# Turning slot rows in place, and the upper heads from 128 B runs, on VectorE instead of TensorE, in a windowed-attention and mixture-of-experts kernel

## The chip, the cores and the metric

The kernel runs on one core of a Trainium2 chip. The metric is device time in microseconds (us). Before the change three runs gave a median of 631.35 us (630.63 to 631.54). The engines are named as the profile names them: PE (TensorE; PEld is its weight load), DVE (VectorE), ACT (ScalarE), POOL (GpSimd) and SP (SyncE, which here only starts transfers). Each has a queue of its own that it works through in order.

## The reference, cut to what matters

```python
# attention: q, k, v are [8 batches, 8 heads, 576 positions, 64]
scores = np.matmul(q, k.transpose(0, 1, 3, 2)) / 8
mask = (rel >= 0) & (rel < 64)               # rel = query position - key position
attn = softmax(np.where(mask, scores, -1e9))
x = np.matmul(attn, v)                       # heads put side by side: [4608, 512]
# mixture of experts: w1 is [8, 512, 1024], w2 is [8, 1024, 512]
logits = x @ w_gate + modality_bias[modality_id]
e_idx = np.argmax(logits, axis=1)
gate_w = softmax(logits)[arange, e_idx]
for e in range(8):
    rows = e_idx == e
    out[rows] = gate_w[rows, None] * (np.maximum(x[rows] @ w1[e], 0) @ w2[e])
```

## The kernel before, in words

**Attention.** The 4608 positions are 72 blocks of 64; two blocks are a *pair* (36 pairs, 128 query rows each), two pairs a *group* (18 groups of four blocks). The main loop `for s in range(NPR + 4)` (L1023) takes one pair a step and holds, written out by hand, the stages of several pairs: scores, minima (L637), exponentials (L649), the turns of the probabilities (`probs_t`, L481), the values (L675), `values_out` (L681 and L683, rows `xa`), the turn of those rows, the logits (L700, and L705, which adds the bias: `lg`) and the route, which scatters each row by its expert into the DRAM tensor `xs_scratch`.

Scores need Q and K with the head dimension on the partitions. They arrive with positions on the partitions, and *heads are turned*: step s turns those of group s//2 + 1, K at even s and Q at odd s, in two parts, `heads[0]` (heads 0 to 3, L1076 to L1079) and `heads[1]` (heads 4 to 7, L1098 to L1101). A part is four PE turns of 128x128 (`heads_t`, through `turn`, L481) into a bank named `tp`, then one copy into `kT` or `qT` (`heads_out`, L588): by ACT for the second part of K, by DVE otherwise. `load_qk` (L563) brings a group's q or k in two transfers of 256 B runs (L574), or in four where the group straddles two batches (groups 11, 13 and 15 among those that matter here). Groups 1 to 7 are loaded ahead into a stock; from 8 on, the loads are issued on SP three steps (k) or two steps (q) ahead of the turns, into two rotating buffers.

**Experts.** Routed rows are processed in *slots* of 256 rows, 18 of them and a half one at the end. A slot needs its rows turned too: x with its 512 columns on the partitions, split into a rounded high part `xh` (ACT, L195) and the rest `xl` (DVE, L196), since each product is made of three matmuls (high by high, low by high, high by low; the weights are split alike into `Whi`, L114 on ACT, and `Wlo`, L119 on DVE, from pieces that SP loads into `y`, L103). `first` (L318) makes the hidden layer, of which ACT takes `hh` (L326) and DVE `hl` (L327); `second` (L340) makes the output `y`, which DVE scales (L348) and POOL scatters (L351).

A generator, `slot_pieces`, cuts a slot into 16 pieces of matmuls. From step FIRST = 12 on, each attention step has four gaps, and `gap` puts one piece into each, so that a slot takes four steps, and PE's order alternates between attention and experts. What ACT and DVE do behind a piece is put into the list `later`, and `run_later` writes it out at fixed places of the step. Behind attention the remaining pieces follow each other (`last` is set).

The next slot's rows are fetched by `fetch` (L250) into `xt`, one buffer, ahead of the piece `first(2, 1)`. Eight slots, the first, six more beside attention and the one just behind it, come by one transfer with rows on the partitions, and PE turns them: `x_turn` (L266, L281), eight turns of 128x128, four into bank `em` ahead of one piece and four into bank `tp` behind another; `x_split` (L285) then makes `xh` and `xl` from PSUM. The seven after the first start their turns at 114.5, 158.1, 201.8, 245.9, 289.4, 331.5 and 361.8 us of the span. The other ten and the half slot, fetched when attention is over, come in *quarters*: four transfers, each 32 partitions wide, and a fifth for the tail (gate weight and row number), so that 32x32 blocks need only be turned in themselves, which is what DVE's transpose does (L276, 128x256 at a time, into PSUM).

PSUM banks are in pools: `tp` is a pool of two (`ps_t`), taken in turn by the head turns, the probability turns, the logits and the slots' second half; `em`, `y0`, `y1`, `sp0` have one bank each.

Of the kernel before, what the change touches and what calls it, by code (L numbers as in the profile page):

```python
# [19 lines left out]
P = 128  # L20
W64 = 64
# [5 lines left out]
def tile_window_attn_moe(  # L27
# [28 lines left out]
    TP = 2 * P  # L56
# [18 lines left out]
    NC1 = DM // P  # L75
# [118 lines left out]
    def split(ps, hi, lo):  # L194
        nc.scalar.copy(out=hi, in_=ps)  # L195
        nc.vector.tensor_tensor(out=lo, in0=ps, in1=hi.bitcast(F32), op=ALU.subtract)  # L196
# [32 lines left out]
    last = []  # L229
    position = [-4]  # L230
# [19 lines left out]
    def fetch():  # L250
        if fetched:
            return fetched.pop(0)
        row, late, buf, whichever, need = todo.pop(0)
        assert late is not None or not pads
        assert late is None or late in scattered
        tick(need - issued[0], table=True)
        nb = 1 if whichever == NANY else 2
        quarters = bool(last)
        xt = load_slot(row, late, nb, quarters)
        return dict(xt=xt, buf=buf, any=whichever, nb=nb, quarters=quarters,  # L260
                    tail=tail_of(xt) if quarters else xt[:, :, DM:])

    def slot_pieces():


        def x_turn(sl, i, tp=None):  # L266

            xt, nb = sl["xt"], sl["nb"]
            if ("tp", i) in sl or nb == 1 and i == 0:
                return  # L270
            tp = sl["tp", i] = tp or bank(2 if i and (last or not sl["quarters"]) else 0)
            cs_ = range(2 * i, 2 * i + 2) if nb == 2 else range(NC1)
            for n, c in enumerate(cs_):
                cols = slice(n * nb * P, (n + 1) * nb * P)
                if sl["quarters"]:
                    nc.vector.transpose(  # L276
                        out=tp[:, cols].rearrange("p (w t) -> p w t", t=R32),
                        in_=x_of(xt)[:, 0:nb, :, :, c].rearrange("p b w d -> p (b w) d"))
                    continue
                for t in range(nb):  # L280
                    nc.tensor.transpose(  # L281
                        out=tp[:, cols][:, t * P:(t + 1) * P].bitcast(F32R),
                        in_=xt[:, t, c:DM:NC1].bitcast(F32R), identity=ident_r)

        def x_split(sl, i):  # L285

            nb = sl["nb"]
            x_turn(sl, i)
# [4 lines left out]
            hi, lo = (x[:, (2 * i * TP if nb == 2 else 0):][:, 0:512] for x in sl["x"])
            split(sl.pop(("tp", i)), hi, lo)
            if i == 1:
                sl["gate"] = epool.tile([P, 2], F32, name="gate", bufs=2)
                nc.gpsimd.tensor_copy(out=sl["gate"][:, 0:nb], in_=sl["tail"][:, 0:nb, 0])
                sl["id"] = epool.tile([P, 2], I32, name="id", bufs=2)
                nc.gpsimd.tensor_copy(out=sl["id"][:, 0:nb], in_=sl["tail"][:, 0:nb, 1])

        def x_part(sl, i, tp=None):
            if not sl["quarters"]:
                x_turn(sl, i, tp)
            later.append(lambda: x_split(sl, i))
# [107 lines left out]
        NK = NC2 // 2  # L412
# [10 lines left out]
        while True:  # L423
            nxt = None
            for k in range(1, NK):
                for i in range(2):
                    if (k, i) == ((1, 0) if last else (2, 1)) or k == 2 and i == 1 and nxt is None:
                        assert todo
                        nxt = fetch()
                    first(sl, k, i)  # L430
                    if k == NK - 1 and i == 0 and last and nxt["quarters"]:
                        later.append(lambda: (x_turn(nxt, 0), x_turn(nxt, 1)))
                    yield
                for t in range(2):
# [69 lines left out]
    def by_group(x):  # L504
        return x.rearrange("p (a h j) i -> p a h j i", a=2, h=HP)
# [49 lines left out]
    def new_qk(G, nm):  # L555
# [4 lines left out]
        else:  # L560
            qk[G, nm] = work.tile([P, 2, H, D], F32, name="qk", bufs=2)

    def load_qk(G, nm, blocks=range(GBLK), dma=nc.sync):  # L563

        t = qk[G, nm]
        x = q if nm == "q" else k
        i = blocks[0]
        while i <= blocks[-1]:
            b, g = divmod(GBLK * G + i, BPB)
            n = min(BPB - g, blocks[-1] + 1 - i)  # L570
            src = x[b, :, g * W64:(g + n) * W64].rearrange("h (p t) d -> p t h d", t=2)
            p0 = i * W64 // 2
            for par in range(2):
                dma.dma_start(out=t[p0:p0 + n * W64 // 2, par], in_=src[:, par])  # L574
            i += n

    def heads_t(G, nm, i, tp):


        src = qk[G, nm].rearrange("p t (h a) d -> p t h (a d)", a=2)  # L580
        for h in range(2):
            for t in range(2):
                n = 2 * h + t
                turn(tp[:, n * P:(n + 1) * P], src[:, t, 2 * i + h])
# [438 lines left out]
    for s in range(NPR + 4):  # L1023
# [70 lines left out]
        if n_gap > 2:  # L1094
            if FIRST <= s < FIRST + 4:
                weights(s)
            gap(it, True)
        if heads:  # L1098
            tp = turn_bank(s)
            heads_t(G, *heads[1], tp)  # L1100
            heads_out(tp, G, *heads[1], nc.scalar.copy if heads[1] == K1 else nc.vector.tensor_copy)  # L1101
# [283 lines left out]
```

## Time and profile before

| | before |
|---|---|
| median of three runs | 631.35 us |
| the profiled execution, of which the profile is | 630.53 us |
| its span, first to last instruction | 628.8 us |
| mean granted TensorE clock | 0.999 |
| PE busy | 611.0 us (97%) |
| DVE busy | 383.9 us (61%) |
| ACT busy | 296.8 us (47%) |
| POOL busy | 136.1 us (22%) |
| DMA | 150230 packets, 88.07 MB |

A row of a group reads: line, engine, operation, output tile <- input tiles, partitions x elements and type, number; then busy time and the mean of one in ns; then the engine's idle time just ahead of these, and what ended most of it. A row of a timeline has the start in us and the duration in us of what stands behind it (xN: N instructions in a row, first start to last end), and in brackets the wait ahead of it and its releaser. Matmuls overlap in the records, so PE is read from start to start. SPq rows are transfers being issued; the time is that of the issuing, not of the data. The chain of waits gives: waiter <- releaser: us, times, longest.

### The profile page before, as it was taken

How to read it: one execution, taken by the hardware profiler on the slowest of the kernel's cores; microseconds unless marked ns; L12 is line 12 of the kernel's file. 1: busy time of each engine (PE TensorE's matmuls, PEld its weight loads, DVE VectorE, ACT ScalarE, POOL GpSimd, SP SyncE). 2: the span in 40 equal slices, each digit the busy share in tenths (PEclk: the TensorE clock that was granted, in tenths of full speed). 3: DMA queues.
4: the chain of work that ended last, by engine and by line, in shares of the span. 5: the costliest groups of instructions: out<-in, count | busy, mean ns of one | idle time of the engine just before them, and what ended most of it. 6: DMA issues, size and time to landing. Idle time of an engine off the chain costs nothing. (4 is left out here: it accounts for less than half of the span.)

```text
span 628.8 us, 17271 instructions
## 1 busy us (share of the span) xinstructions
PE 611.0 (97%) x6429; PEld 549.2 (87%) x6429; DVE 383.9 (61%) x1493; ACT 296.8 (47%) x933; POOL 136.1 (22%) x315
## 2 busy tenths in 40 slices
PE   8899799999999999999999999999999999999996
PEld 5788688989898899989898899999899999989986
DVE  4899878766676765656655266324434743876721
ACT  4899785656556554645553111111113522564411
POOL 5423412222222320320323130011011011101102
PEclk9999999999999999999999999999999999999999
DMA  9999846675467544452412132732332653578300
GB/s 177 220 240 242 236 123 181 173 200 171 111 163 194 143 120 103 136 152 60 127 53 85 51 102 71 217 118 67 85 118 76 191 165 96 190 244 252 112 11 27
DMA packets 150230, 88.07 MB, mean 140 GB/s; under 512 B 120010, under 2 KB 130816, under 8 KB 150016
## 3 DMA queue, kind: packets, MB, share of 16 engines
q1 hardware_dynamic: 141568, 67.45, 41.6%
q0 software_dynamic: 5888, 18.93, 8.0%
q8 instruction: 51, 0.84, 0.5%
q10 hardware_dynamic: 2688, 0.58, 0.5%
q14 instruction: 35, 0.29, 0.2%
HBM read 67.49 MB, written 23.91 MB: 145 GB/s over the span
## 5 line engine op out<-in xcount | busy, mean ns | idle before, releaser
L340 PE MATMUL y<-Whi,hh 128*128 128x512 f32 x288 | 117.0, 406 | 0.0
L649 ACT ACTIVATE ss<-ss,mn 128x128 f32<-128x128 f32 x288 | 112.6, 398 | 2.0 <-DVE mn L637 2.0
L340 PE MATMUL y<-Wlo,hh 128*128 128x512 f32 x288 | 112.7, 391 | 0.0
L340 PE MATMUL y<-Whi,hl 128*128 128x512 f32 x288 | 112.6, 391 | 0.0
L351 POOL DMA_INDIRECT out_dram<-y,id x36 | 37.4, 1040 | 248.3 <-DVE y L348 165.4
L327 DVE SCALAR_TENSOR_TENSOR hl<-em,hh 128x512 fp32r<-128x512 f32 x50 | 34.5, 690 | 92.3 <-ACT hh L326 89.6
L318 PE MATMUL em<-xh,Whi 128*128 128x256 f32 x400 | 83.7, 291 | 0.0
L326 ACT ACTIVATE hh<-em 128x512 fp32r<-128x512 f32 x50 | 29.6, 593 | 106.1 <-PE em L318 102.1
L318 PE MATMUL em<-xl,Whi 128*128 128x256 f32 x400 | 79.3, 279 | 0.0
L318 PE MATMUL em<-xh,Wlo 128*128 128x256 f32 x400 | 79.2, 279 | 0.0
L637 DVE CUSTOM_DVE_ANT_0 ss<-sp,masks 128x128 f32<-128x128 f32 x288 | 63.6, 286 | 11.9 <-PE sp L623 10.5
L658 ACT COPY pT<-tp 128x512 f32<-128x512 f32 x57 | 31.4, 590 | 74.7 <-PE tp L481 74.0
L340 PEld LDWEIGHTS y<-Whi,hl 128*128 128x128 f32 x288 | 54.1, 188 | 12.2
L318 PEld LDWEIGHTS em<-xh,Whi 128*128 128x128 f32 x400 | 62.3, 189 | 2.0 <-DVE xl L196 0.2
L340 PEld LDWEIGHTS y<-Whi,hh 128*128 128x128 f32 x288 | 54.2, 188 | 8.2
L340 PEld LDWEIGHTS y<-Wlo,hh 128*128 128x128 f32 x288 | 54.2, 188 | 7.8
L318 PEld LDWEIGHTS em<-xl,Whi 128*128 128x128 f32 x400 | 60.9, 188 | 0.0
L318 PEld LDWEIGHTS em<-xh,Wlo 128*128 128x128 f32 x400 | 60.9, 188 | 0.0
L649 ACT ACTIVATION_READ_ACCUMULATOR ss<-ss,mn 128x1 f32 x288 | 56.1, 195 | 0.0
L776 POOL DMA_INDIRECT xs_scratch<-xa,idx x36 | 36.4, 1012 | 82.5 <-DVE lm L719 27.2
L326 ACT ACTIVATE hh<-sp 128x512 fp32r<-128x512 f32 x22 | 13.2, 598 | 76.0 <-PE sp L318 74.0
L675 PEld LDWEIGHTS av<-ve,pT 128*64 128x64 f32 x576 | 36.3, 138 | 12.1 <-issue 5.7
(251 smaller groups left out, 1231.0 us busy)
## 6 DMA issues: line engine op xcount, KB each, us to landing
vo<-in_v_dram SPq DMA_DIRECT2D x32, 256.0 KB
y<-in_moe_w_dram SPq DMA_DIRECT2D x32, 256.0 KB
vo<-in_moe_w_dram SPq DMA_DIRECT2D x24, 256.0 KB
ss<-in_moe_w_dram SPq DMA_DIRECT2D x24, 256.0 KB
xt<-xs_scratch SPq DMA_DIRECT2D x40, 128.0 KB
xt<-xs_scratch SPq DMA_DIRECT2D x8, 514.0 KB
xs_scratch<-xs_scratch SPq DMA_DIRECT2D x8, 514.0 KB
pT<-in_moe_w_dram SPq DMA_DIRECT2D x16, 256.0 KB
```

Of the source, the lines that this page charges most:

```text
L318: nc.tensor.matmul(out=hb[:, i * TP:(i + 1) * TP], lhsT=w[buf][:, c0:c0 + P], rhs=x[:, c * TP:(c + 1) * TP], start=(n == 0), stop=(n == le ...
L326: nc.scalar.activation(out=hh, in_=hb, func=AF.Relu),
L327: nc.vector.scalar_tensor_tensor(out=hl, in0=hb, scalar=0.0, in1=hh.bitcast(F32), op0=ALU.max, op1=ALU.subtract)))
L340: nc.tensor.matmul(out=sl["y", t], lhsT=h[:, i * TP + t * P:i * TP + (t + 1) * P], rhs=w[buf][:, c0:c0 + DM], start=(k == 0 and n == 0), s ...
L351: ins = nc.gpsimd.indirect_dma_start(out=out, out_offset=bass.IndirectOffsetOnAxis(ap=sl["id"][:, t:t + 1], axis=0), in_=y, in_offset=None ...
L637: nc.vector.tensor_tensor_reduce(out=ss[a][:, hp, :], in0=sp[a][:, hp * P:(hp + 1) * P], in1=mask, scale=-1.0 / 8.0, scalar=3.0e38, op0=AL ...
L649: nc.scalar.activation(out=ss[a][:, hp, :], in_=ss[a][:, hp, :], func=AF.Exp, bias=mn[:, h:h + 1], scale=-1.0, accum_out=sm[:, h:h + 1])
L658: nc.scalar.copy(out=pT, in_=pp)
L675: nc.tensor.matmul(out=av[c * W64:(c + 1) * W64, 2 * hp + a], lhsT=pT[:, i:i + W64], rhs=(vo if c else ve)[p][:, 2 * hp + a, :], start=Tru ...
L776: ins = nc.gpsimd.indirect_dma_start(out=xs, out_offset=bass.IndirectOffsetOnAxis(ap=idx[:, j:j + 1], axis=0), in_=xg[j], in_offset=None)
```

## The change

**Slot rows.** `quarters` is now true for every slot but the first, so the seven slots named above also load by five transfers instead of one. PE no longer turns their rows. `x_turn` turns a whole slot in place in `xt`, SBUF to SBUF, by two DVE transposes of 128x512; it is queued in `later` behind `first(3, 1)` (in the tail, where DVE turned already, behind `first(3, 0)`). `xh` and `xl` are made from `xt` and no longer from PSUM.

**Heads.** For groups 8 to 17 (QUARTERS = 8; turned at steps 14 to 33) heads 0 to 3 are loaded and turned as before, from one half of the tile. Heads 4 to 7 are loaded into its other half by eight transfers, one for each head and 32-column half, each 32 partitions wide in runs of 128 B. `turn_heads` then makes `kT` or `qT` by a single DVE transpose of 128x512, in the place where four PE turns and a copy stood. A q or k load is ten transfers instead of two, twenty instead of four where the group straddles two batches.

```diff
-        quarters = bool(last)
+        quarters = bool(position[0] > 0)
...
-        def x_turn(sl, i, tp=None):
+        def x_turn(sl):
+            blocks = x_of(sl["xt"])[:, 0:sl["nb"]].rearrange("p b w d c -> p (b w) c d")
+            for c in range(0, NC1, 2):
+                nc.vector.transpose(out=blocks[:, :, c:c + 2], in_=blocks[:, :, c:c + 2])
...
+            if sl["quarters"]:
+                tp = x_of(xt)[:, 0:nb].rearrange("p b w t c -> p c (b w) t")[:, cs_]
+                hi, lo = (x.rearrange("p (c w t) -> p c w t", w=nb * NR, t=R32) for x in (hi, lo))
+            else:
+                tp = tp or bank(2 if i else 0)
...
-                    if k == NK - 1 and i == 0 and last and nxt["quarters"]:
-                        later.append(lambda: (x_turn(nxt, 0), x_turn(nxt, 1)))
+                    if k == NK - 1 and i == (0 if last else 1) and nxt["quarters"]:
+                        later.append(lambda: x_turn(nxt))
...
+    QUARTERS = 8
...
+    def turn_heads(G, nm, i):
+        dst = by_group(qT if nm == "q" else kT)[:, G % 2, 2 * i:2 * i + 2]
+        nc.vector.transpose(
+            out=dst.rearrange("p h j i -> p (h j i)"),
+            in_=by_heads(qk[G, nm]).rearrange("p h u d -> p (h u d)"))
...
+            nh = H if G < QUARTERS else HP
...
+            for h in range(nh, H):
+                for c in range(2):
+                    rows = slice((h % 2 * 2 + c) * R32, (h % 2 * 2 + c + 1) * R32)
+                    src = x[b, h, g * W64:(g + n) * W64, c * R32:(c + 1) * R32]
+                    dma.dma_start(out=by_heads(t)[rows, (h - nh) // 2, u, :],
+                                  in_=src.rearrange("(u p) d -> p u d", p=R32))
...
-        if heads:
+        if heads and G >= QUARTERS:
+            turn_heads(G, *heads[1])
+        elif heads:
             tp = turn_bank(s)
             heads_t(G, *heads[1], tp)
```

How this moves instructions is shown at the fifth of the seven slots that change (its turns start at 289.4 us before). Lines behind the change are numbered anew: L340 is L334 after, L327 is L321, L705 is L723, L574 is L585 and L591. DVE before; `cnt`, `tgt`, `se`, `dst` and the two reciprocals are the route's, `xl` the slot's low part:

```order
L327 SCALAR_TENSOR_TENSOR hl<-em,hh 128x512
L801 COPY cnt<-tp 1x8
L757 TENSOR_TENSOR tgt<-tp,ebase 128x16
L588 COPY qT<-tp 128x2x2x128
L762 TENSOR_REDUCE se<-ex 128x2
L763 TENSOR_TENSOR tgt<-tgt,oh 128x16
L764 TENSOR_SCALAR se<-se 128x2
L766 TENSOR_REDUCE dst<-tgt 128x2
L770 RECIPROCAL xa_102<-se 128x1
L770 RECIPROCAL xa_103<-se 128x1
L196 TENSOR_TENSOR xl<-em,xh 128x512
L196 TENSOR_TENSOR xl<-tp,xh 128x512
```

DVE in the same place after:

```order
L321 SCALAR_TENSOR_TENSOR hl<-em,hh 128x512
L270 STREAM_TRANSPOSE xt<-xt 128x8x2x32 x2
L819 COPY cnt<-tp 1x8
L775 TENSOR_TENSOR tgt<-tp,ebase 128x16
L569 STREAM_TRANSPOSE qT<-qk 128x512
L780 TENSOR_REDUCE se<-ex 128x2
L781 TENSOR_TENSOR tgt<-tgt,oh 128x16
L782 TENSOR_SCALAR se<-se 128x2
L784 TENSOR_REDUCE dst<-tgt 128x2
L788 RECIPROCAL xa_102<-se 128x1
L788 RECIPROCAL xa_103<-se 128x1
L196 TENSOR_TENSOR xl<-xt,xh 128x512 x2
```

Two slot turns stand ahead of the route's small operations, the copy of Q has become a turn, and both `xl` read `xt`. Behind both come `rs`, `xa` and `lg` (L681, L683 and L705 before). On PE, at the same slot, before (`y_5162` and `y_5181` are two output banks of the experts; the numbers only tell tiles apart):

```order
L340 MATMUL y_5162<-Whi_2480,hh 128x512
L340 MATMUL y_5162<-Wlo_67,hh 128x512
L340 MATMUL y_5162<-Whi_2480,hl 128x512
L481 MATMUL tp<-ident_r,qk 128x128 x4
L281 MATMUL em<-ident_r,xt 128x128 x4
L340 MATMUL y_5181<-Whi_2480,hh 128x512
L340 MATMUL y_5181<-Wlo_67,hh 128x512
L340 MATMUL y_5181<-Whi_2480,hl 128x512
```

PE there after:

```order
L334 MATMUL y_5255<-Whi_2505,hh 128x512
L334 MATMUL y_5255<-Wlo_67,hh 128x512
L334 MATMUL y_5255<-Whi_2505,hl 128x512
L334 MATMUL y_5269<-Whi_2505,hh 128x512
L334 MATMUL y_5269<-Wlo_67,hh 128x512
L334 MATMUL y_5269<-Whi_2505,hl 128x512
```

The turns of the second pair of heads and the first four of the slot are gone, and one piece follows the other. On SP, group 11's k load (it straddles two batches), between a load of v and the expert weights, before:

```order
L103 DMA y<-in_moe_w_dram 128x512
L539 DMA vo<-in_v_dram 128x8x64
L574 DMA qk<-in_k_dram 32x8x64 x2
L574 DMA qk<-in_k_dram 96x8x64 x2
L103 ISA
L103 DMA y<-in_moe_w_dram 128x512
```

The same place on SP after:

```order
L103 DMA y<-in_moe_w_dram 128x512
L534 DMA vo<-in_v_dram 128x8x64
L585 DMA qk<-in_k_dram 32x4x64 x2
L591 DMA qk<-in_k_dram 32x2x32 x8
L585 DMA qk<-in_k_dram 96x4x64 x2
L591 DMA qk<-in_k_dram 32x6x32 x8
L103 ISA
L103 DMA y<-in_moe_w_dram 128x512
```

Four issues became twenty, and the next piece of weights stands behind all of them.

More of the change, by code (lines that the diff above doesn't have):

```diff
@@ L263, in slot_pieces, with x_part @@
     def slot_pieces():
-        def x_turn(sl, i, tp=None):
-            xt, nb = sl["xt"], sl["nb"]
[L269 to L288, printed above, removed]
+        def x_turn(sl):
+            blocks = x_of(sl["xt"])[:, 0:sl["nb"]].rearrange("p b w d c -> p (b w) c d")
+            for c in range(0, NC1, 2):
+                nc.vector.transpose(out=blocks[:, :, c:c + 2], in_=blocks[:, :, c:c + 2])
+        def x_part(sl, i, tp=None):
+            xt, nb = sl["xt"], sl["nb"]
             if i == 0:
@@ L292, in x_split, with out_ @@
                     return
[L293 to L304, printed above, removed]
+            cs_ = slice(2 * i, 2 * i + 2) if nb == 2 else slice(0, NC1)
+            hi, lo = (x[:, cs_.start * nb * P:][:, 0:512] for x in sl["x"])
+            if sl["quarters"]:
[3 more added lines that the diff above has]
+                tp = tp or bank(2 if i else 0)
+                for n, (c, t) in enumerate((c, t) for c in range(cs_.start, cs_.stop) for t in range(nb)):
+                    nc.tensor.transpose(
+                        out=tp[:, n * P:(n + 1) * P].bitcast(F32R), in_=xt[:, t, c:DM:NC1].bitcast(F32R),
+                        identity=ident_r)
+            def out_():
+                split(tp, hi, lo)
+                if i == 1:
+                    sl["gate"] = epool.tile([P, 2], F32, name="gate", bufs=2)
+                    nc.gpsimd.tensor_copy(out=sl["gate"][:, 0:nb], in_=sl["tail"][:, 0:nb, 0])
+                    sl["id"] = epool.tile([P, 2], I32, name="id", bufs=2)
+                    nc.gpsimd.tensor_copy(out=sl["id"][:, 0:nb], in_=sl["tail"][:, 0:nb, 1])
+            later.append(out_)
         def first(sl, k, i):
@@ L561, in new_qk, with plain, by_heads @@
             qk[G, nm] = work.tile([P, 2, H, D], F32, name="qk", bufs=2)
+    def plain(t, nh):
+        return t.rearrange("p t h d -> p (t h d)")[:, 0:2 * nh * D].rearrange("p (t h d) -> p t h d", t=2, d=D)
+    def by_heads(t):
+        return t.rearrange("p t h d -> p (t h d)")[:, H * D:].rearrange("p (h u d) -> p h u d", h=HP // 2, d=R32)
+    def turn_heads(G, nm, i):
[3 more added lines that the diff above has]
+            in_=by_heads(qk[G, nm]).rearrange("p h u d -> p (h u d)"))
     def load_qk(G, nm, blocks=range(GBLK), dma=nc.sync):
@@ L570, in load_qk @@
             n = min(BPB - g, blocks[-1] + 1 - i)
-            src = x[b, :, g * W64:(g + n) * W64].rearrange("h (p t) d -> p t h d", t=2)
+            nh = H if G < QUARTERS else HP
+            src = x[b, 0:nh, g * W64:(g + n) * W64].rearrange("h (p t) d -> p t h d", t=2)
             p0 = i * W64 // 2
             for par in range(2):
-                dma.dma_start(out=t[p0:p0 + n * W64 // 2, par], in_=src[:, par])
+                dma.dma_start(out=plain(t, nh)[p0:p0 + n * W64 // 2, par], in_=src[:, par])
+            u = slice(i * W64 // R32, (i + n) * W64 // R32)
+            for h in range(nh, H):
[4 more added lines that the diff above has]
+                                  in_=src.rearrange("(u p) d -> p u d", p=R32))
             i += n
     def heads_t(G, nm, i, tp):
-        src = qk[G, nm].rearrange("p t (h a) d -> p t h (a d)", a=2)
+        src = plain(qk[G, nm], H if G < QUARTERS else HP).rearrange("p t (h a) d -> p t h (a d)", a=2)
         for h in range(2):
```

## The prediction

> **What bounds the kernel now.** I read the page first, then the busy time by stretches, then the timelines of TensorE (PE), VectorE (DVE), ScalarE (ACT) and the SP queue around the instructions that change. The page's sums:
>
> ```profile
> PE 611.0 (97%) x6429; PEld 549.2 (87%) x6429; DVE 383.9 (61%) x1493; ACT 296.8 (47%) x933; POOL 136.1 (22%) x315
> ```
>
> Busy time by stretches, one with attention and one behind it (columns: span, then PE, PEld, DVE, ACT, POOL, granted clock, DMA share, GB/s):
>
> ```profile
> 230.00:275.00 45.00, 44.98 (x575) 40.82 (x575) 28.36 (x151) 24.95 (x92) 10.76 (x22) 1.00 0.45 120
> 400.00:480.00 80.00, 80.00 (x519) 72.80 (x519) 29.52 (x45) 12.46 (x23) 8.71 (x23) 1.00 0.37 107
> ```
>
> PE has no idle time worth the name in either, and the clock is full. So work taken off PE shortens the run, unless another queue then makes PE wait. DVE is busy 63% of the attention stretch (28.36 of 45), in order, and receives nearly all the new work; that is where I look for the wait.
>
> **What a turn costs PE.** Four turns of a Q or K tile (L481), then the y matmuls; a step without slot turns:
>
> ```profile
> 278.41 0.60 PE L481 MATMUL tp<-ident_r,qk 128*128 128x128 f32 x4
> 278.76 0.48 PE L340 MATMUL y<-Whi,hh 128*128 128x512 f32 x1
> 279.08 0.40 PE L340 MATMUL y<-Wlo,hh 128*128 128x512 f32 x1
> 279.31 0.40 PE L340 MATMUL y<-Whi,hl 128*128 128x512 f32 x1
> ```
>
> PE is read by start times, because busy times overlap. The four turns hold it 0.35 us (278.41 to 278.76), and the matmul behind them takes 0.32 instead of 0.23 to its successor, so four turns cost 0.44. The second pair of heads is taken off PE for k and q of ten groups: 20 x 0.44 = 8.8 us. Now a step in which a slot's rows are turned too (I call it an x-step; this is the fifth of the seven that change):
>
> ```profile
> 288.84 0.39 PE L340 MATMUL y<-Whi,hl 128*128 128x512 f32 x1
> 289.07 0.60 PE L481 MATMUL tp<-ident_r,qk 128*128 128x128 f32 x4
> 289.42 0.74 PE L281 MATMUL em<-ident_r,xt 128*128 128x128 f32 x4
> 290.00 0.46 PE L340 MATMUL y<-Whi,hh 128*128 128x512 f32 x1
> ...
> 291.46 0.63 PE L281 MATMUL tp<-ident_r,xt 128*128 128x128 f32 x4
> 292.02 0.27 PE L675 MATMUL av<-ve,pT 128*64 128x64 f32 x1
> ...
> 294.56 0.66 PE L481 MATMUL tp<-ident_r,ss 128*128 128x128 f32 x4
> ```
>
> The slot's eight turns hold PE 0.58 + 0.56 = 1.14 us; seven slots give 8.0. If PE never waited more than today, 8.8 + 8.0 = 16.8 us would go: 613.7. That is the floor.
>
> **What the same work costs DVE.** The new turns are 128x512, SBUF to SBUF; the trace has shorter ones that write PSUM (L276), and plain passes over 512 elements (mean ns behind the comma):
>
> ```profile
> L276 DVE STREAM_TRANSPOSE em<-xt 128x256 f32<-128x256 f32 x20 | 12.9, 645 | 1.6 <-DMA xt<-xs_scratch 1.1
> L276 DVE STREAM_TRANSPOSE tp<-xt 128x128 f32<-128x128 f32 x4 | 1.7, 419 | 0.1
> L119 DVE TENSOR_TENSOR Wlo<-y,Whi 128x512 fp32r<-128x512 f32 x32 | 21.8, 682 | 1.1 <-ACT Whi L114 0.9
> L588 DVE COPY qT<-tp 128x512 f32<-128x512 f32 x27 | 18.5, 690 | 22.4 <-PE tp L481 22.3
> ```
>
> From 128 to 256 elements a turn grows by 0.21 to 0.23 us; a line through the two gives 1.04 to 1.10 at 512. The other bound is the plain SBUF pass, 0.68. I take 1.07, since the operation and the strided read are the same, and 0.99 from start to start (neighbours on DVE overlap by about 0.08: in the rows below, 289.70 + 0.69 is 290.39, and the next starts at 290.31). DVE loses the Q copy (0.69, 0.61 start to start) and ACT the K copy.
>
> In steps without a slot DVE's extra 0.4 to 1.0 us falls into waits for PE that it has today (22.4 us in front of L588's q copies alone), so I cost it at nothing; what is uncovered if that goes is the same wait as below. In an x-step it doesn't. DVE there, today:
>
> ```profile
> 288.32 0.68 DVE L327 SCALAR_TENSOR_TENSOR hl<-em,hh 128x512 fp32r<-128x512 f32 x1
> ...
> 289.70 0.69 DVE L588 COPY qT<-tp 128x512 f32<-128x512 f32 x1 [0.56 <-PE tp L481]
> 290.31 0.16 DVE L762 TENSOR_REDUCE se<-ex 128x2 f32<-128x16 f32 x1
> ...
> 290.85 0.67 DVE L196 TENSOR_TENSOR xl<-em,xh 128x512 fp32r<-128x512 f32 x1
> 292.75 0.69 DVE L196 TENSOR_TENSOR xl<-tp,xh 128x512 fp32r<-128x512 f32 x1 [1.23 <-ACT xh L195]
> 293.36 0.19 DVE L681 RECIPROCAL rs<-rs 128x8 f32<-128x8 f32 x1
> 293.64 0.69 DVE L683 TENSOR_TENSOR xa<-av,rs 128x512 f32<-128x512 f32 x1
> 294.25 0.16 DVE L705 TENSOR_TENSOR lg<-tp,bias_sel 128x8 f32<-128x8 f32 x1
> ```
>
> PE waits for the last of these. The logits lie in one of two rotating tp banks, the first four probability turns take the other, and the second four need the logits' bank back. The trace has that wait already:
>
> ```profile
> PEld tp L481 <- DVE lg L705: 3.7, 9, 1.4
> 336.63 0.63 PE L481 MATMUL tp<-ident_r,ss 128*128 128x128 f32 x4 [0.37 <-DVE lg L705]
> ```
>
> New chain in the fifth x-step: hl leaves DVE at 288.93; two slot turns 1.98; cnt and tgt 0.15; the Q turn 0.99; five small ones 0.54 (290.31 to 290.85); two xl at 0.61; rs 0.28; xa 0.61; lg 0.16. It ends at 294.86. ACT's two xh lie under the Q turn. PE gains 1.16 - 0.23 = 0.93 from 288.84 to 290.00, 0.09 at the slow matmul behind, and 0.56 at 291.46: 1.58. It would start the second four at 294.56 - 1.58 + 0.35 = 293.33, and waits until 294.86; today they start at 294.91. **The x-step gives back what it gained: about 0.** The fourth is alike (no weight split in the chain either). The first three also hold weight splits (Wlo) in that chain; the first of them:
>
> ```profile
> 113.74 0.69 DVE L327 SCALAR_TENSOR_TENSOR hl<-em,hh 128x512 fp32r<-128x512 f32 x1 [0.30 <-ACT hh L326]
> ...
> 114.43 0.68 DVE L119 TENSOR_TENSOR Wlo<-y,Whi 128x512 fp32r<-128x512 f32 x1
> ...
> 116.17 0.67 DVE L119 TENSOR_TENSOR Wlo<-y,Whi 128x512 fp32r<-128x512 f32 x1
> ...
> 119.65 1.09 PE L481 MATMUL tp<-ident_r,ss 128*128 128x128 f32 x8
> ```
>
> There lg ends at 114.35 + 1.98 + 0.08 + 0.60 + 0.99 + 0.54 + 0.59 + 1.22 + 0.28 + 0.61 + 0.16 = 121.40, against 120.00 today: 1.4 lost. The second and third have one Wlo in the chain: 0.8 lost each. The sixth has no Q turn; its chain ends 0.3 before today's 336.63. The seventh has no attention behind it and keeps 1.1.
>
> **Loads.** Issues on SP (time taken by a run of issues), and ACT at the first x-step:
>
> ```profile
> 107.84 4.25 SPq L574 DMA_DIRECT2D qk<-in_k_dram  x2
> 112.35 3.23 SPq L103 DMA_DIRECT2D y<-in_moe_w_dram  x3
> 115.55 0.62 ACT L114 CAST Whi<-y 128x512 fp32r<-128x512 f32 x1 [0.18 <-DMA y<-in_moe_w_dram]
> 194.76 3.97 SPq L574 DMA_DIRECT2D qk<-in_k_dram  x4
> 471.27 2.50 SPq L214 DMA_DIRECT2D xt<-xs_scratch  x5
> 212.96 0.60 PE L481 MATMUL tp<-ident_r,qk 128*128 128x128 f32 x4
> ```
>
> A slot load becomes five issues (2.50 us, 2.1 more), a q or k load ten instead of two, or twenty instead of four where the group straddles two batches. The last row is where PE turns the second pair of heads of group 13's k, which the load at 194.76 brings. A piece of weights issued at 112.35 is what ACT waits for until 115.55, so a landing takes about 3.2 us. Behind a slot load of five and a k load of ten (10 x 0.50 = 5.0 against 4.25) that piece comes 2.9 us later; ACT's xh stand behind it, and of this about 0.5 reaches lg. Elsewhere the loads have a step of slack (about 10 us) and cost nothing. With 128 B runs the bytes stay the same, and the DMA engines, 0.45 busy above, have room.
>
> Behind attention DVE turns a slot in two instructions (1.98) instead of four of 645 or so; PE is full there (80.00 of 80), so nothing comes of it.
>
> **The sum.** Five of the twenty head turns stand in x-steps and are counted there; the other 15 x 0.44 = 6.6; x-steps -1.4 - 0.8 - 0.8 + 0 + 0 + 0.3 + 1.1 = -1.6; late weights -0.5: 4.5 us gained. The profiled execution took 630.53 (span 628.8), 0.82 below the median of the runs, 631.35; the same gain on the median gives **626.9**.
>
> **Rivals.** *Short turns.* If the slope of the turns comes from writing PSUM, a 512 turn costs as a plain SBUF pass, 0.68, or 0.61 start to start. Each chain is then 1.14 shorter: x-steps -0.3, +0.3, +0.3, +1.2, +1.2, +1.1, +1.1, with the late weights 4.4 instead of -2.1, and 11.0 in all: 620.3. For it: SBUF on both sides, and a dense read for q and k. Against it: both lengths in the trace have the steep slope. The Trainium skill ("Vector Engine (DVE) Microarchitecture Reference", 3.8) says that the 32x32 array sustains one element per cycle and lane; by that rule, at its 0.96 GHz, a 512 turn is an estimated 0.53 us of stream and this rival is the case. The trace's rows disagree so far: 128 more elements take 0.23 us, not 0.13.
>
> *Late loads, slower.* Group 13's k load starts behind five slot issues, at 196.9. To land (3.2) by 212.96 its twenty issues have 12.9 us, 0.64 each; they decide from there. The rows give 0.50 (471.27) and 0.99 (194.76, large ones). At 0.8 each DVE stands 3.1 us in front of the last turn with all of its queue behind it: the bank of the logits, then the minima that ACT waits for. Three such groups, k and q: 18.6 us, less the 4.5: 645. For it: the issues at 194.76. Against it: sixteen of the twenty new ones carry an eighth of those each. The Trainium skill ("DMA: Bandwidth & Descriptors", Specifications) wants at least 512 B in a transfer for full rate, which speaks against 128 B runs and for this rival. Today's runs of 256 B are below that too, at a DMA share of 0.45, so the trace does not bear it out so far.
>
> *Nothing moves.* A late minima in x-steps delays exponentials and so the next step too; 0.7 more in each of six takes the gain away: 631.
>
> **Chances.** Forecast 0.47, short turns 0.23, late loads 0.15, nothing moves 0.15. A difference under 0.2% (1.3 us) can't be told by a measurement of this kernel. Faster 0.69 (both gains, less the forecast's near edge), same 0.15, slower 0.16. The range runs from 617, which takes in the short turns though not the floor, to 634, where late loads begin: 0.20 left out, mostly above.
>
> **What would show it.** Right: STREAM_TRANSPOSE 128x512 near 1.07 us; PE's wait for lg L705 (there under a new line) grown from 3.7 to about 10 us, at steps with slot turns; attention's steps without slots 0.44 shorter. Short turns: 0.7 us, and little wait. Late loads: DVE waits for DMA before its turns, above all at groups 11, 13 and 15. The forecast is wrong if PE waits at the slot steps for something else than lg, or if the steps without slots don't shorten.

## The result, and the profile after

The changed kernel takes 638.1 us (637.2 to 639.3, four runs) where the kernel before took 631.1 on the same chips: a ratio of 1.011, with an interval of 1.0095 to 1.0125. It is slower by 7 us; the forecast was 626.9, in a range of 617 to 634. The page of the changed kernel, its sums and the row of the granted clock:

```profile
PE 602.0 (95%) x6293; PEld 536.7 (84%) x6293; DVE 412.7 (65%) x1495; ACT 311.3 (49%) x923; POOL 136.9 (22%) x315
...
PEclk7999999999899999999999999999999999999999
```

PE has 9 us less to do and the span, 636.3, is 7.5 longer: PE now waits. Of the clock's digits the 7 at the start comes and goes between executions, as step 0 does (below); the 8 stands at 159 to 175 us. The two stretches that were shown of before, after the change (span, PE, PEld, DVE, ACT, POOL, clock, DMA share, GB/s):

```profile
230.00:275.00 45.00, 40.15 (x525) 35.08 (x526) 31.18 (x145) 21.90 (x77) 10.85 (x22) 1.00 0.53 122
400.00:480.00 80.00, 80.00 (x527) 73.09 (x526) 29.20 (x35) 14.43 (x20) 8.62 (x22) 1.00 0.39 118
```

The stretch behind attention is as full as it was; in attention PE idles 4.85 us of 45, where it idled 0.02. What PE waits for between 110 and 362 us (us in total, times, longest):

```profile
PE tp L475 <- ACT pT L676: 8.9, 6, 4.4
PE tp L475 <- DVE lg L723: 7.4, 4, 2.6
PE tp L475 <- DMA qk<-in_q_dram: 1.6, 2, 1.3
```

All but the last row are the second four probability turns (the forecast's place), waiting for the logits' bank (`lg`) or for ACT's copy of the first four (`pT`); which of the two depends on the bank that the pool hands out. The groups of the changed operations (mean ns behind the comma):

```profile
L195 ACT CAST xh<-xt 128x512 fp32r<-128x512 f32 x35 | 37.7, 1127 | 4.9 <-DVE xt L270 4.6
L196 DVE TENSOR_TENSOR xl<-xt,xh 128x512 fp32r<-128x512 f32 x35 | 36.4, 1075 | 5.5 <-ACT xh L195 5.5
L270 DVE STREAM_TRANSPOSE xt<-xt 128x512 f32<-128x512 f32 x34 | 36.1, 1114 | 1.1 <-DMA xt<-xs_scratch 0.9
L569 DVE STREAM_TRANSPOSE kT<-qk 128x512 f32<-128x512 f32 x10 | 7.1, 711 | 1.9 <-issue 1.0 <-DMA qk<-in_q_dram 0.6 <-DMA qk<-in_k_dram 0.4
L569 DVE STREAM_TRANSPOSE qT<-qk 128x512 f32<-128x512 f32 x10 | 7.0, 696 | 2.7 <-DMA qk<-in_q_dram 2.7
```

A slot's turn in place takes 1.11 us and a turn of heads 0.70. Both splits of `xt` have become dearer: `xl` 1.07 where it took 0.68 to 0.69 from PSUM, `xh` 1.13 where it took 0.59.

Where the time went is best read step by step, from the first score matmul of a pair to that of the next one (L623 before, L641 after; the rows are PE's timeline). A slot is turned in steps 15, 19, 23, 27 and 31; its wait for `lg` falls behind the next scores, so into the step that follows, and the two are put together. Span in us:

| steps | before | after | difference |
|---|---|---|---|
| up to 11 | 74.1 | 75.3 | +1.2 |
| 12, 13, 14, 17, 18, 22, 30, 33, 34 (no slot turn) | | | -3.4 in all |
| 15 + 16, first slot | 22.2 | 27.1 | +4.9 |
| 19 + 20, second slot | 22.2 | 24.2 | +2.0 |
| 23 + 24, third slot | 22.2 | 21.3 | -0.9 |
| 27 + 28, fourth slot | 22.2 | 22.8 | +0.6 |
| 31 + 32, fifth slot | 22.2 | 22.0 | -0.1 |
| 21 and 29 | 21.8 | 23.3 | +1.5 |
| 25 and 26 (q of group 13) | 21.9 | 25.0 | +3.1 |
| from 35 on, with the sixth and seventh slot | 304.4 | 303.0 | -1.4 |

The first row is none of the change's: step 0 takes 3.8 to 3.9 us in nine and 5.4 to 5.7 in five of the fourteen executions profiled here, of kernels that do the same there.

**The fifth slot** is the one that the forecast worked through. DVE there, after the change:

```profile
297.80 0.68 DVE L321 SCALAR_TENSOR_TENSOR hl<-em,hh 128x512 fp32r<-128x512 f32 x1
298.40 2.12 DVE L270 STREAM_TRANSPOSE xt<-xt 128x512 f32<-128x512 f32 x2
...
300.51 0.70 DVE L569 STREAM_TRANSPOSE qT<-qk 128x512 f32<-128x512 f32 x1
...
301.67 2.06 DVE L196 TENSOR_TENSOR xl<-xt,xh 128x512 fp32r<-128x512 f32 x2
303.65 0.20 DVE L699 RECIPROCAL rs<-rs 128x8 f32<-128x8 f32 x1
303.93 0.69 DVE L701 TENSOR_TENSOR xa<-av,rs 128x512 f32<-128x512 f32 x1
304.54 0.16 DVE L723 TENSOR_TENSOR lg<-tp,bias_sel 128x8 f32<-128x8 f32 x1
```

and PE, which had its first four probability turns done at 303.20:

```profile
304.84 0.63 PE L475 MATMUL tp<-ident_r,ss 128*128 128x128 f32 x4 [1.65 <-DVE lg L723]
```

The chain runs without a hole from `hl` to `lg`, and PE gives back what it gained: -0.1 for both steps, where the forecast had 0 for the slot and 0.4 for the head turn that step 32 no longer has. Inside the chain two errors cancel in part: the Q turn is 0.36 shorter than forecast (0.63 to the next start, not 0.99), the two `xl` are 0.8 longer (1.98, not 1.22).

**The first slot.** SP's issues, then ACT, PE and the granted clock:

```profile
106.87 2.45 SPq L214 DMA_DIRECT2D xt<-xs_scratch  x5
109.61 0.36 SPq L107 DMA_DIRECT2D y<-in_moe_w_dram  x1
110.54 0.34 SPq L103 DMA_DIRECT2D y<-in_moe_w_dram  x1
111.00 1.10 SPq L534 DMA_DIRECT2D vo<-in_v_dram  x1
112.20 1.07 SPq L585 DMA_DIRECT2D qk<-in_k_dram  x2
113.33 4.00 SPq L591 DMA_DIRECT2D qk<-in_k_dram  x8
117.58 1.95 SPq L103 DMA_DIRECT2D y<-in_moe_w_dram  x3
```

```profile
121.04 0.62 ACT L114 CAST Whi<-y 128x512 fp32r<-128x512 f32 x1 [4.90 <-DMA y<-in_moe_w_dram]
121.56 2.10 ACT L195 CAST xh<-xt 128x512 fp32r<-128x512 f32 x2
123.57 0.57 ACT L676 COPY pT<-tp 128x512 f32<-128x512 f32 x1
```

```profile
124.19 1.12 PE L475 MATMUL tp<-ident_r,ss 128*128 128x128 f32 x4 [4.37 <-ACT pT L676]
124.96 0.78 PE L334 MATMUL y<-Whi,hh 128*128 128x512 f32 x1
```

```profile
118.00:124.00 6.00, 1.34 (x24) 0.84 (x20) 2.94 (x10) 2.96 (x4) 0.00 (x0) 1.00 0.88 227
124.00:128.00 4.00, 3.81 (x15) 3.20 (x15) 3.86 (x22) 1.61 (x6) 0.00 (x0) 0.57 0.39 64
...
169.00:172.00 3.00, 2.89 (x9) 2.51 (x10) 2.07 (x17) 1.36 (x5) 0.00 (x0) 0.52 0.51 108
```

The weights that were issued at 112.35 are issued at 117.58, behind five slot and ten k issues (1.2 us of the difference was there before the slot's load, which starts at 106.87 instead of 105.63). ACT waits for them 4.9 us, in order, with both `xh` and the copy of the probabilities behind it; PE waits 4.4. Then the clock is granted at 0.57 for 4 us, another 1.7 us of PE's time. The last row is the same behind the second slot's wait (2.59 us): 0.52 for 3 us, 1.4 more.

**Group 13.** Its k and q are loads of twenty issues each, and the queue is behind already when they begin:

```profile
206.02 1.27 SPq L585 DMA_DIRECT2D qk<-in_k_dram  x2
207.34 4.72 SPq L591 DMA_DIRECT2D qk<-in_k_dram  x8
212.11 1.26 SPq L585 DMA_DIRECT2D qk<-in_k_dram  x2
213.42 3.93 SPq L591 DMA_DIRECT2D qk<-in_k_dram  x8
...
220.50 1.54 SPq L585 DMA_DIRECT2D qk<-in_q_dram  x2
222.09 5.52 SPq L591 DMA_DIRECT2D qk<-in_q_dram  x8
227.66 1.26 SPq L585 DMA_DIRECT2D qk<-in_q_dram  x2
228.96 5.07 SPq L591 DMA_DIRECT2D qk<-in_q_dram  x8
```

```profile
235.47 0.71 DVE L569 STREAM_TRANSPOSE qT<-qk 128x512 f32<-128x512 f32 x1 [2.71 <-DMA qk<-in_q_dram]
```

From 206.0 to 234.0 SP issues two loads and little else, 28 us; the two steps in which they are issued, 23 and 24, take 21. The queue cannot keep up, and DVE (2.7 us) and PE (1.6) wait for q.

**Steps 21 and 29** turn q of groups 11 and 15, also loads of twenty, but no wait for a load stands there. PE waits for ACT's copy of the first four probability turns, and ACT just ahead of that copy waits for PE:

```profile
181.86 0.66 PE L475 MATMUL tp<-ident_r,ss 128*128 128x128 f32 x4 [1.26 <-ACT pT L676]
...
272.65 0.66 PE L475 MATMUL tp<-ident_r,ss 128*128 128x128 f32 x4 [1.28 <-ACT pT L676]
```

Before the change the eight turns of step 21 followed each other without a wait. Both fours want the same bank, it seems; no run tests that.

### The profile page after: what moved, and what is told of

Read it like the earlier page. It is cut to its first block, busy times and chain, and to the rows that moved or that the text cites. A ratio compares the mean times of both kernels' runs of the same rounds, so it can differ in the third digit from the quotient of the medians.

```text
span 636.3 us, 17393 instructions
## 1 busy us (share of the span) xinstructions
PE 602.0 (95%) x6293; PEld 536.7 (84%) x6293; DVE 412.7 (65%) x1495; ACT 311.3 (49%) x923; POOL 136.9 (22%) x315
## 4 chain that ended last, share of the span: by engine, by line
PE 50%; DVE 1%; issue 0%; ACT 0%; POOL 0%; POOLq 0%; DVEq 0%
PE y L334 22%; PE em L312 13%; PE sp L312 10%; PE tp L475 2%; PE y L385 1%; PE av L693 1%; PE sp L641 0%; PE sp L360 0%; PE em L360 0%; PE tp L718 0%; DVE xt L270 0%; DVE xl L196 0%; POOL out_dram L398 0%; DVE xa L701 0%; ACT hh L320 0%
## 5 line engine op out<-in xcount | busy, mean ns | idle before, releaser
L334 PE MATMUL y<-Whi,hh 128*128 128x512 f32 x288 | 116.2, 403 | 0.0
L334 PE MATMUL y<-Wlo,hh 128*128 128x512 f32 x288 | 113.5, 394 | 0.0
L334 PE MATMUL y<-Whi,hl 128*128 128x512 f32 x288 | 112.9, 392 | 0.0
L321 DVE SCALAR_TENSOR_TENSOR hl<-em,hh 128x512 fp32r<-128x512 f32 x50 | 34.5, 690 | 79.8 <-ACT hh L320 75.0
L334 PEld LDWEIGHTS y<-Whi,hl 128*128 128x128 f32 x288 | 54.6, 190 | 12.2
L334 PEld LDWEIGHTS y<-Whi,hh 128*128 128x128 f32 x288 | 54.6, 190 | 8.9
L334 PEld LDWEIGHTS y<-Wlo,hh 128*128 128x128 f32 x288 | 54.7, 190 | 8.6
L794 POOL DMA_INDIRECT xs_scratch<-xa,idx x36 | 36.4, 1012 | 77.9 <-DVE lm L737 22.8
L475 PE MATMUL tp<-ident_r,ss 128*128 128x128 f32 x236 | 36.4, 287 | 17.3 <-ACT pT L676 8.9
```

Source lines behind the costliest of these rows:

```text
L321: nc.vector.scalar_tensor_tensor(out=hl, in0=hb, scalar=0.0, in1=hh.bitcast(F32), op0=ALU.max, op1=ALU.subtract)))
L334: nc.tensor.matmul(out=sl["y", t], lhsT=h[:, i * TP + t * P:i * TP + (t + 1) * P], rhs=w[buf][:, c0:c0 + DM], start=(k == 0 and n == 0), s ...
L475: nc.tensor.transpose(out=out_, in_=in_, identity=ident[p0:p0 + n, p0:p0 + n])
L794: ins = nc.gpsimd.indirect_dma_start(out=xs, out_offset=bass.IndirectOffsetOnAxis(ap=idx[:, j:j + 1], axis=0), in_=xg[j], in_offset=None)
```

## The experiments

Two theories were set against each other and against a mixture: D, DVE's longer chain in the slot steps; L, the SP queue with its 236 more issues; M, both. Each ratio is to the kernel before, on the same chip. In the table are the median, the ratio with its interval, and the spans of the steps in question in the profiled execution, which is one of the runs and need not be the median one (xl_late's took 624.3):

| kernel | us | ratio | 15+16 | 19+20 | 23+24 | 25 | 26 | 27+28 | 31+32 |
|---|---|---|---|---|---|---|---|---|---|
| before | 631.1 | 1 | 22.2 | 22.2 | 22.2 | 11.5 | 10.5 | 22.2 | 22.2 |
| after | 638.1 | 1.0110 (1.0095 to 1.0125) | 27.1 | 24.2 | 21.3 | 13.7 | 11.3 | 22.8 | 22.0 |
| heads_only | 629.6 | 0.9973 (0.9957 to 0.9989) | 25.9 | 21.8 | 21.8 | 11.4 | 10.0 | 21.4 | 21.3 |
| rows_only | 635.6 | 1.0061 (1.0041 to 1.0082) | 23.1 | 23.4 | 25.4 | 11.4 | 10.5 | 22.5 | 22.5 |
| weights_first | 634.8 | 1.0056 (1.0032 to 1.0079) | 27.1 | 21.3 | 22.8 | 12.8 | 11.3 | 22.1 | 22.0 |
| loads_only | 643.1 | 1.0174 (1.0144 to 1.0204) | 28.3 | 22.2 | 22.2 | 17.2 | 10.5 | 22.2 | 22.2 |
| heads_weights | 623.8 | 0.9895 (0.9876 to 0.9914) | 21.9 | 21.7 | 21.8 | 11.1 | 10.0 | 21.4 | 21.4 |
| loads_weights | 637.1 | 1.0116 (1.0095 to 1.0137) | 23.2 | 22.2 | 22.8 | 15.7 | 10.5 | 22.2 | 22.2 |
| dense_split | 633.2 | 1.0043 (1.0018 to 1.0068) | 28.5 | 23.8 | 21.1 | 15.9 | 10.0 | 21.3 | 21.2 |
| dense_weights | 631.8 | 1.0029 (1.0009 to 1.0049) | 26.7 | 21.0 | 26.3 | 11.7 | 11.2 | 21.3 | 21.2 |
| xl_late | 628.5 | 0.9975 (0.9956 to 0.9993) | 22.4 | 21.2 | 22.1 | 12.9 | 11.5 | 20.3 | 20.3 |
| xl_after | 628.1 | 0.9973 (0.9950 to 0.9997) | 23.3 | 21.2 | 23.8 | 12.8 | 11.7 | 20.3 | 20.3 |
| heads_weights_tail | 624.2 | 0.9906 (0.9886 to 0.9925) | 21.9 | 21.8 | 21.7 | 12.4 | 10.0 | 21.4 | 21.4 |
| xl_late_plain | 625.2 | 0.9913 (0.9890 to 0.9937) | 24.2 | 21.7 | 21.7 | 11.6 | 10.0 | 20.7 | 20.3 |

### One part alone, and the issues alone

heads_only leaves the slots beside attention as they were, rows_only the heads:

```diff
-        quarters = bool(position[0] > 0)
+        quarters = bool(last)          # heads_only
...
-    QUARTERS = 8
+    QUARTERS = NG                      # rows_only
```

> Only the heads part: slots beside attention are loaded by one transfer and turned by PE as before. Theory D (the loss is DVE's chain in the slot steps, above all the splits of xt, 1.07 us each on DVE and 1.13 on ACT where PSUM took 0.68 and 0.59): the heads part keeps nearly all of its 8.8 us, 624. Theory L (the loss is the SP queue: 208 of the 236 new issues are those of heads): 635 or more. My own, M, holds that both count: 8.8 gained, about 4 lost where group 13's q load comes late (DVE waited 2.7 and PE 1.6 us for it) and little at the first slot, 627 to 628.

> Only the rows part: heads are loaded and turned by PE in all groups. D: each slot step loses what DVE's chain is longer, about 636. L: 28 issues more and 8 us of PE work less, about 624. M: the first two slot steps lose (late weights, long chain), the next four are even, the seventh gains 1: 633.

loads_only is the kernel before with the changed kernel's number of issues and all turns on PE (its slots come in five transfers too; the diff shows the loads of q and k):

```diff
-                dma.dma_start(out=t[p0:p0 + n * W64 // 2, par], in_=src[:, par])
+                dma.dma_start(out=t[p0:p0 + n * W64 // 2, par, 0:nh], in_=src[:, par, 0:nh])
+            for h in range(nh, H):
+                for par in range(2):
+                    dma.dma_start(out=t[p0:p0 + n * W64 // 2, par, h:h + 1], in_=src[:, par, h:h + 1])
```

> The kernel before with the changed kernel's number of issues and nothing else: q and k of groups 8 to 17 in ten or twenty transfers of 256 B runs, slots in five, PE turns everything. D: 631, the queue has room. L: 640 or more. M: 636, from the late piece of weights at the first slot (about 3) and group 13's q (about 2 to 3).

Measured: 629.6, 635.6 and 643.1. Neither pure theory holds. The heads part gains 1.8 of its 8.8; the rows part, with few new issues, loses 4.2, so L alone is out; the issues alone, with no new work on DVE, lose 11.7, so D alone is out. D's figure fits rows_only and L's loads_only; M, the author's own, is out by about 2 to 7 us in all three, and had one place wrong: heads_only should have lost 4 us at group 13's late q. It loses them at the first slot (25.9 where heads_weights, below, takes 21.9), and steps 25 and 26 take 21.4 although group 13's loads are the same twenty issues each. They start at 199.18, 2.9 us into step 23 (5.5 in the changed kernel, behind five slot issues), and PE does not wait for q:

```profile
227.58 0.71 DVE L569 STREAM_TRANSPOSE qT<-qk 128x512 f32<-128x512 f32 x1 [0.91 <-DMA qk<-in_q_dram]
```

Loads_only shows the two places of the queue bare. ACT at its first slot:

```profile
122.68 0.62 ACT L114 CAST Whi<-y 128x512 fp32r<-128x512 f32 x1 [6.38 <-DMA y<-in_moe_w_dram]
```

and PE in its step 25, where the q of group 13 is turned:

```profile
236.59 0.30 PE L485 MATMUL tp<-ident_r,qk 128*128 128x128 f32 x1 [1.79 <-DMA qk<-in_q_dram]
```

These steps lose 6.1 and 5.8 us and step 21 another 1.2; the other slots lose nothing. The runs are still 256 B there, so the number of issues can do it without the 128 B.

### Weights ahead of the load

One load, group 9's k, moves behind the pieces of weights of its step, in the changed kernel (weights_first), in heads_only (heads_weights) and in loads_only (loads_weights):

```diff
-            when(step, load_qk, G, nm)
+            when(step + (0.5 if (G, nm) == (9, "k") else 0), load_qk, G, nm)
...
         if s >= WEIGHTS:
             weights(s)
+        for f, args in at.pop(s + 0.5, ()):
+            f(*args)
```

> The changed kernel with one load moved: group 9's k (ten issues, 5 us) behind the pieces of weights of its step on SP. The piece that ACT waited for until 121.0 us should land about 5 us sooner, and xh, xl and lg of the first slot step with it. L and M: 633 (638.1 less 5). D: no change, 637 to 638.

> Heads part only, with group 9's k behind the weights of its step on SP. Theory M (the late piece of weights holds ACT, ACT's xh and with them PE at the first slot; PE's pause then halves the clock for some 4 us): heads_only lost 4.1 us against its neighbours in that step, which should go: 629.6 less 4 is 625.6, faster than the kernel before. Rival: the step is held by what else DVE has there (the turn of q instead of the copy), and the time stays at 629 to 630.

> loads_only (issues of the changed kernel, work of the kernel before) with group 9's k behind the weights of its step. M: the 6.1 us that loads_only lost in the step of the first slot go, 643.1 less 6 is 637; group 13's late q (5.8 us in its step) stays. Rival (the slot's own five issues or the 256 B packets make the weights late, not the ten issues of k): 642 to 643.

Measured 634.8, 623.8 and 637.1. In heads_weights and loads_weights the first slot's steps fall by 4.0 and 5.1 us, and ACT hardly waits for the weights. ACT's cast of them in heads_only, and in heads_weights:

```profile
119.03 0.62 ACT L114 CAST Whi<-y 128x512 fp32r<-128x512 f32 x1 [4.01 <-DMA y<-in_moe_w_dram]
```

```profile
114.77 1.13 ACT L114 CAST Whi<-y 128x512 fp32r<-128x512 f32 x2
```

Heads_weights is faster than both kernels: 0.9895 of the kernel before. In weights_first the total came out near the figure expected, but not for the reason: its first slot still takes 27.1 us, and the profiled gain lies elsewhere (2.9 us in 19 + 20, where the half clock stayed away, and 1.2 before step 12, which is not the edit's; 23 + 24 takes 1.5 back). The weights were in time, and PE waited for two other things, by its place the Q turn (the row names `se`, which stands right behind it on DVE) and `lg`:

```profile
118.13 0.67 PE L641 MATMUL sp<-kT,qT 64*64 64x128 f32 x16 [1.33 <-DVE se L780]
122.24 1.09 PE L475 MATMUL tp<-ident_r,ss 128*128 128x128 f32 x4 [2.85 <-DVE lg L723]
```

So at the first slot, with the whole change, two causes lie side by side, late weights and DVE's chain, and each alone is long enough for the pause and the halved clock behind it.

### Splits that read in a row

```diff
-                tp = x_of(xt)[:, 0:nb].rearrange("p b w t c -> p c (b w) t")[:, cs_]
-                hi, lo = (x.rearrange("p (c w t) -> p c w t", w=nb * NR, t=R32) for x in (hi, lo))
+                tp = xt.rearrange("p b c -> p (b c)")[:, (512 * i if nb == 2 else 0):][:, 0:512]
```

dense_split is the changed kernel with this, dense_weights has group 9's k moved as well. Both leave out the order of x's columns, so they show a time and compute something else.

> The changed kernel, whose xh and xl read xt in a row instead of every fourth element; columns of x then meet the wrong rows of w1, so the experts' products are not the reference's, while routing, sizes and all else stay. D: xl falls from 1.07 to 0.68 and xh from 1.13 to 0.59, DVE's chain in a slot step is 0.8 shorter and ACT's 1.1; five slot steps at 0.8 to 1.1 and the half clock of the second slot's (1.9) give 638.1 less 5 to 7: 631 to 633. L (issues alone): 637 to 638.

> Both of the last edits in the changed kernel: dense reads of xt (products not the reference's, as in dense_split) and group 9's k behind the weights. If the late weights and the strided splits are separate terms, their gains add: weights_first gained 3.3, dense_split gains 5 to 7, so 628 to 630. If the first slot's step stays long as it did in weights_first (16.9 us), DVE's turns alone hold it, and the sum falls short by 4.

Measured 633.2 and 631.8. The groups of dense_split between 110 and 362 us, DVE and then ACT:

```profile
L196 DVE TENSOR_TENSOR xl<-xt,xh 128x512 fp32r<-128x512 f32 x12 | 8.1, 718 | 4.5 <-ACT xh L195 4.4
```

```profile
L195 ACT CAST xh<-xt 128x512 fp32r<-128x512 f32 x12 | 6.8, 615 | 6.4 <-DVE xt L270 5.2 <-DVE tgt L774 1.1
```

The strided read costs 0.36 us an `xl` and 0.51 an `xh`. Without it the changed kernel is 4.9 us faster (against 638.1; 4.2 by the two ratios, each on its own chip), of which 1.5 and 0.8 lie in the fourth and fifth slot. Dense_weights misses its expected sum by 2 to 4: its first slot stays at 26.7, as the second case of its expectation had it, and its third slot waited for its rows (DVE 2.6 us for the load of `xt`).

### xl out of the chain

weights_first, with `xl` run behind `lg`:

```diff
+                if late_lo:
+                    lows.append(low)
+                else:
+                    low()
...
+            if lows:
+                lows.pop(0)()          # xl_late only: the first half ahead of the minima
             minima(s)
...
+        while lows:
+            lows.pop(0)()
```

As written this is xl_late, one half of `xl` on each side of the minima. xl_after leaves out the first pop, so that both halves come behind the minima; its expectation names another place (both ahead of them), which is not what ran.

> weights_first (the whole change, group 9's k behind the weights) with xl taken out of the chain in front of lg: in slots beside attention its first half comes behind lg and ahead of the minima, its second half behind the minima. Theory D (PE waits at the slot steps for the end of DVE's chain, hl, slot turns, q turn, xl, rs, xa, lg): the chain is 2.1 us shorter, the waits of 1 to 3 us for lg at five slot steps and a half clock go, 634.8 less 6 to 8: 627 to 629. Rival (PE waits for the turn of q, or ACT's copies behind two xh of 1.13): 633 or more. If xl then comes late for the slot's first matmuls, PE waits there about 0.5 us a slot instead.

> As xl_late, but both halves of xl stand behind lg and ahead of the minima. D: lg early as in xl_late, the minima and exponentials 2.1 us later than there: about the same time, 627 to 630. If the exponentials were what PE waits for, it would be 3 or more above xl_late.

Measured 628.5 and 628.1. Where no load is late, a slot's two steps fall to 20.3 (fourth and fifth slot: 2.4 and 1.7 below the changed kernel, 1.8 to 1.9 below the kernel before), and the first slot's to 22.4. Nothing but the place of two passes on DVE has changed against weights_first: the wait for `lg` is what the rows part cost at these slots. Whether one half stands ahead of the minima or behind makes no difference that can be told. The rows part still does not pay: heads_weights, without it, is faster (0.9895 beside 0.9975). Where the median run of xl_late loses these 5 us is not known, since its profile is of a run of 624.3.

### The loads of twenty issues, and the last two slots

xl_late_plain is xl_late with groups 11, 13 and 15 loaded and turned as before:

```diff
+    def by_head(G):
+        return G >= QUARTERS and GBLK * G // BPB == (GBLK * G + GBLK - 1) // BPB
...
-        if heads and G >= QUARTERS:
+        if heads and by_head(G):
```

> xl_late with the three groups that straddle two batches (11, 13 and 15) loaded in four transfers and turned by PE as before, so no load has twenty issues. PE gets 6 x 0.44 = 2.6 us back. Theory M (group 13's q, twenty issues, comes late): the three steps around it, 36.4 us together in xl_late where their kind takes 31 to 32, lose 4 to 5, net 2 less: 628.5 to about 626. Rival (those steps are long for another reason, such as the slot's rows): 631, the PE work added and nothing gained.

Measured 625.2. Steps 24, 25 and 26 take 33.2 us instead of 36.4, although PE has turns back, and DVE no longer waits for q there. Steps 21 and 29, whose loads of twenty are gone too, take 23.4 instead of 22.1: they were not long for their loads. The profiled run as a whole is 0.9 us longer than xl_late's (625.2 and 624.3); the gain in all is that of the ratios, 0.9913 beside 0.9975. In xl_late DVE did wait:

```profile
226.49 0.71 DVE L579 STREAM_TRANSPOSE qT<-qk 128x512 f32<-128x512 f32 x1 [2.90 <-DMA qk<-in_q_dram]
```

heads_weights_tail gives heads_weights the rows part for the sixth and seventh slot:

```diff
-        quarters = bool(last)
+        quarters = bool(last or position[0] > 96)
```

> heads_weights with the rows part for the last two of the seven slots alone, whose steps hold no turn of q (the sixth) or no attention (the seventh). In the changed kernel the stretch of these two was 1.4 us shorter than before, in rows_only 0.9: 623.8 less 1 is 622.7. Rival: nothing measurable, 623.8.

Measured 624.2, a ratio of 0.9906 beside 0.9895: no difference that can be told, which is the rival's case. In its profile the stretch from step 35 on is 0.5 us shorter (303.9 instead of 304.4).

## Why the prediction was wrong

**What held.** The price on PE: steps without slot turns are 0.46 to 0.53 us shorter with a head turn gone, as the 0.44 said. One part of the new wait: PE's wait for `lg` went from 2.1 to 8.2 us over the whole run, mostly at the slot steps (the 3.7 that the prediction gives is a row of PEld, the weight load, and counts differently). But PE also waited 9.5 us for ACT's copy `pT` (1.0 before), 4.4 of it at the first slot, and that is the sign by which the prediction called itself wrong. The turn in place: 1.11 against 1.07.

**What agrees by luck.** The third to fifth slot, with the head turns of steps 24, 28 and 32: -0.4 measured, and 0.8 - 1.3 = -0.5 forecast; but slot by slot it is -0.9, +0.6 and -0.1, where +0.4, -0.4 and -0.4 were forecast. (The first two were forecast at +1.5 and +0.4 on the same count, and came to +4.9 and +2.0.) The sixth and seventh: 1.4 gained from step 35 on, as the two terms said, but heads_weights_tail, which has these two alone, shows 0.5.

**First failure, the one that costs most by itself: "Elsewhere the loads have a step of slack (about 10 us) and cost nothing", and for the first slot "2.9 us later ... of this about 0.5 reaches lg".** The weights came 5.5 us later (ACT's cast at 121.04 instead of 115.55; 1.2 of it came from ahead of the slot's load), and it reached PE nearly whole, in a wait of 4.4 us, since `xh` and the probability copy stand behind that cast on ACT. Loads_only has no other change and loses 6.1 us there; moving one load takes 5.1 back. In the changed kernel itself the same move takes nothing back at this slot, since DVE's chain holds PE there as long (27.1 us in weights_first too). The slack of the other loads was read from a queue with two or four issues each. At 0.57 (k) to 0.68 us (q) an issue, group 13's two loads, with the weights and the v between them, need 28 us in two steps of 21 together: what is missing adds up from load to load and eats the slack. Heads_only shows how near it is: there they need 27.0 us in 21.8, begin earlier, and PE does not wait. Group 13's k was forecast to start at 196.9 and started at 206.0, of which 6.4 is that its step 23 itself began later (200.56 instead of 194.18). This was the rival of late loads, given 0.15; its place (group 13) and its sign were right, its rule was not. At 0.57 an issue k stayed below the 0.64 from which the rival was said to decide, and came nearly in time; q, behind it, did not. The bound looked at one load that starts on time. The description ahead of the prediction has loads issued three and two steps ahead of the turns; by the code it is one step, for k and for q, which is also the slack that the prediction gives.

**Second failure: a term of the sum.** `xl` was costed at 0.61 and `xh` was hidden; they take 1.07 and 1.13, because `xt` turned in place is read at every fourth element. The diff's pattern shows that, and the prediction passed over it. Dense_split measures it: 1.5 and 0.8 us at the fourth and fifth slot. The Trainium skill ("SBUF — State Buffer", Specifications (TRN2)) has lines of 16 bytes, at least two hits in each for full rate; four f32 is one hit a line. The trace agrees with a loss, 1.07 to 0.72 on DVE and 1.13 to 0.62 on ACT. The prediction could have used that page and did not.

**Third failure: what a wait costs.** Waits were costed at their length. Pauses of 2.1 to 4.5 us were followed in several kernels by 3 to 4 us at half the clock. The changed kernel has that twice, 1.7 + 1.4 = 3.1 us, beside a forecast gain of 4.5. The Trainium skill ("TensorE: Matmul & The Clock Gate", Why this matters for your kernels) warns of gaps over about 3 us; here 2.12 us sufficed once (heads_only), while 2.27 in the changed kernel's fourth slot did not, so that the measured pauses decide, and they give no threshold.

**Short turns.** The head turn took 0.70 us, which is that rival's value, and the slot turn 1.11, which is the forecast's: both have the same number of elements, but the first is read and written in a row and the second at every fourth element, in place. No run separates the stride from the turning in place. The estimate of 0.53 us for 512 that the prediction took from the Trainium skill ("Vector Engine (DVE) Microarchitecture Reference", 3.8) is reached by neither.

**Added up** (profiled executions, +7.5): start +1.2; the first slot +4.9 and the second +2.0, with the two half clocks; steps 25 and 26, with group 13's late q, +3.1; steps 21 and 29 +1.5; third to fifth slot -0.4; other steps -3.4; from step 35 on, with the sixth and seventh slot, -1.4. That 25 and 26 are long for the loads is tested (xl_late_plain). The cause of 21 and 29 stays open: loads_only loses 1.2 in step 21 and nothing in step 29, and both stay long in xl_late_plain, without their loads of twenty. What is shown there is the wait for ACT's copy, 1.26 and 1.28 us.

## What to carry to other kernels

Count what a change adds to a transfer queue as a rate against the stretch it must fit in, and not only as a delay against the slack of today; and look for what stands behind it in order, on the queue and on the engine that waits. When work leaves the busiest engine for another, write out that engine's chain at the step where both are full, with the access pattern of every operation that reads the new layout, and then move out of the chain what nobody needs there: two passes moved behind `lg` and one load behind the weights turned 638.1 into 628.5 (1.0110 into 0.9975 of the kernel before), and the same load moved with the rows part left out gave 623.8 (0.9895).

## What the runs showed of the hardware

An issue takes SP about the same time whatever its size: in the changed kernel eight transfers of 8 KB took 3.71 and 4.08 us (group 11), eight of 16 KB 3.93 to 5.52 (group 13), eight of 32 KB 4.00 to 5.87 (groups 9 and 12). DVE's passes with a source at every fourth f32 took 1.07 us for 128x512 against 0.72 in a row, ACT's 1.13 against 0.62. After a pause of PE the clock was often granted at 0.5 for 3 to 4 us (6.8 in weights_first), and sometimes not: a pause of 2.51 us in rows_only was followed by it, one of 2.15 there was not. Shorter pauses can do it together: 0.97 and 0.91 us, 1.3 apart, in xl_late_plain's first slot were followed by 3.4 us at 0.50, while 0.53 and 0.91 at the same place in xl_late were not.

```profile
120.10:123.50 3.40, 3.40 (x12) 2.71 (x11) 3.37 (x19) 1.36 (x5) 0.00 (x0) 0.50 0.53 90
```
